# Weight narrowing moved from GpSimd to VectorE at other paces, and the sums of squares placed behind the last score product, in a channel-attention and GELU feed-forward kernel

## The chip, the cores and the metric

The kernel runs on one core of one Trainium2 chip. The metric is the time of one execution in microseconds (us) of device time; shorter is better. A core has TensorE (PE, matrix products; PEld is its loading of weights), VectorE (DVE), ScalarE (ACT), GpSimd (POOL) and SyncE (SP), which issues all DMAs of this kernel. Each engine works through its own queue of instructions in order.

## The reference

```python
def _attn_ref(q, k, v, tau):                      # each (4, 6080, 256)
    qn = q / (np.linalg.norm(q, axis=1, keepdims=True) + 1e-06)
    kn = k / (np.linalg.norm(k, axis=1, keepdims=True) + 1e-06)
    s = kn.transpose(0, 2, 1) @ qn / tau          # 256 x 256 per batch
    s = s - s.max(-1, keepdims=True)
    a = np.exp(s)
    a /= a.sum(-1, keepdims=True) + 1e-09
    return v @ a

def _moe_ref(x, w_in, w_out):                     # w_in 256 x 2048, w_out 2048 x 256
    h = x @ w_in
    g = 0.5 * h * (1.0 + erf(h / np.sqrt(2.0)))
    return g @ w_out
```

The attention runs over the 256 channels, so the scores are 256 x 256 per batch, and the norms are taken over the 6080 tokens. Its output, 24320 rows of 256, goes through the feed-forward layer. The weights arrive as 64-bit floats.

## The kernel before, in words

**Stages.** For each of 4 batches there is a score stage, a softmax, and 6 pairs of token tiles of up to 512 columns. For a pair, 8 steps (u = 0 to 7) go over the 2048 hidden channels. The attention matrix is multiplied into `w_in` beforehand (`w_group`, four groups g of 512 hidden channels, 12 products each), so that a step takes the tokens of `v` directly. Almost all products work on a high and a low part of each operand (`wh` and `wl`, `vh` and `vl`, `gh` and `gl`), three products each.

**A step.** `first_products` (lines 448 to 450) makes seven products of three matmuls; their results are copied by ScalarE (`p` and `u`, line 468), added by VectorE (`h`, line 473), and go through ScalarE's GELU twice (`gh` and `g`, lines 456 and 457), and VectorE takes the low part (`gl`, line 458). `second_products` (lines 518 to 520) multiplies the step's result with `w_out`; the second products of step u run between the first products of step u+1. TensorE does 21 + 24 matmuls in a step.

**The score stage of batch 0.** 24 loads `raw` of keys and queries (512 KB each, 13 buffers) come from `qk`, with the 24 sets of score products in `qk_first` (line 147, four matmuls of two passes each). For the first 16 of them ScalarE squares the load (`sq`, line 136, two buffers) and VectorE adds it to `acc` (line 137). The rest of the sum of squares comes from 8 pieces of the transposed keys and queries (`kqt`, line 211, three buffers), squared and summed by ScalarE (line 212). SyncE issues all of these loads from one queue in the order of the program, so a load that waits for its buffer holds up those behind it. Eight small matmuls against a column of ones (`sum_up`, line 175) add `acc` over the partitions. Four loads of batch 1 follow, and their score products (`qk_fill`, line 164) are what TensorE does in the gaps of the first softmax; `GAPS` says how many in each gap.

**The narrowing.** The 16 units of the weights (8 of `w_in`, 8 of `w_out`, 128 x 512 each) are turned from 64-bit floats into a high and a low part by integer and float operations on the two 32-bit words (`narrow`, lines 237 to 258): a clip (line 237, VectorE), a square (239, ScalarE), shifting and joining of the bits (242, 244, VectorE), a masked product (246, VectorE), an exponent mask (249, VectorE), the tail from the low word, the high part `hi` (256, ScalarE's copy), and the rest `lo` (257 and 258). Of these GpSimd does lines 257 and 258 for every unit, and line 255 of the tail for 12 units; for the other 4, VectorE makes the tail in one operation (line 251). Five units are narrowed in or right behind the score loop (`NARROWS`), though the order that comes out has two of these in the first softmax; one more follows it, and ten are spread over the first pair's steps, as many behind each step as `paces` says. Each unit is then written to DRAM (`keep`, line 551) for the later pairs and batches, and its place in the load queue goes to the next unit's load.

**What sets the order.** The program is written in one order, and instructions are placed on each engine's queue by a scheduler with priorities; `behind(...)` makes an instruction come after a marked one.

Of the kernel before, what the change touches and what calls it, by code (L numbers as in the profile page):

```python
# [9 lines left out]
F32 = mybir.dt.float32  # L10
F32R = mybir.dt.float32r
U32 = mybir.dt.uint32
AF = mybir.ActivationFunctionType
ALU = mybir.AluOpType
AX = mybir.AxisListType

P = 128
B, N, C = 4, 6080, 256
DFF = 2048
NT = 512  # L20
NJ = -(-N // P)
NFT = DFF // P
NCT = C // P
# [21 lines left out]
NARROWS = (4, 7, 12, 18, 20)  # L45

GAPS = (7, 4, 2)

VEC = 3

TOP_MAX = (2.0 - 2.0 ** -3 - 2.0 ** -23) * 2.0 ** 16
TOP_MIN = 1.125 * 2.0 ** -15
# [6 lines left out]
def channel_attention_gelu_ffn(ctx, tc, qk, kqt, vt, tau, w_in, w_out, out):  # L59
# [30 lines left out]
    def f32(ap):  # L90
        return ap.bitcast(F32)
# [48 lines left out]
    def qk_first(js):  # L140
        if js == 0:
            state["s"] = [bank()[:, 0:C] for m in range(NCT)]
        s = state["s"]
        raw = raws.pop((0, js))
        for j in range(JS):
            for m in range(NCT):
                nc.tensor.matmul(s[m], raw[:, j, 0, m * P:(m + 1) * P], raw[:, j, 1],
                                 start=(js == 0 and j == 0), stop=(js * JS + j == NJ - 1), skip_group_check=True)
        if js < NSQ:
            squares(js, raw)  # L150
        if js == NSQ + 2:
            nps, acc = ps_o.tile([P, NT], F32, name="po"), state.pop("acc")
            for j in range(JS):
                sum_up(nps, acc[:, j], j == 0, j == JS - 1)
            state["nps"] = nps


    def qk_fill():
        state["fill"] = s = ps_o.tile([P, NCT, C], F32, name="po")
# [61 lines left out]
        nc.sync.dma_start(out=raw, in_=src.bitcast(U32).rearrange("p (n w) -> p n w", w=2))  # L221
        return raw

    def narrow(hi, lo, raw, eng):


        n = raw.shape[1]
        low, high = raw[:, :, 0], raw[:, :, 1]

        if "filled" not in state:  # L230
            tmp = pst.tile([P, 2, n], F32, name="nt", bufs=2)
        else:
            tmp = pg.tile([P, 2, n], F32, name="kqc", bufs=2)

        top = high.bitcast(F32)
        body, w, tail = tmp[:, 0].bitcast(U32), tmp[:, 0], tmp[:, 1]
        nc.vector.tensor_scalar(out=top, in0=high.bitcast(F32), scalar1=TOP_MAX, scalar2=-TOP_MAX,
                                op0=ALU.min, op1=ALU.max)
        nc.scalar.activation(out=tail, in_=top, func=AF.Square)

        topu = top.bitcast(U32)
        nc.vector.tensor_scalar(out=body, in0=topu, scalar1=0x07FFFFFF, scalar2=3,
                                op0=ALU.bitwise_and, op1=ALU.logical_shift_left)
        nc.vector.scalar_tensor_tensor(out=topu, in0=topu, scalar=0xC0000000, in1=body,
                                       op0=ALU.bitwise_and, op1=ALU.bitwise_or)
        nc.vector.scalar_tensor_tensor(out=w, in0=tail, scalar=TOP_MIN ** 2, in1=top, op0=ALU.is_ge, op1=ALU.mult)

        body = high
        nc.vector.tensor_scalar(out=body, in0=w.bitcast(U32), scalar1=0xFF800000, scalar2=None, op0=ALU.bitwise_and)
        if eng is nc.vector:  # L250
            eng.scalar_tensor_tensor(out=tail, in0=low, scalar=2.0 ** -52, in1=body.bitcast(F32), op0=ALU.mult,
                                     op1=ALU.mult)
        else:
            nc.scalar.activation(out=tail, in_=low, func=AF.Copy, scale=2.0 ** -52)
            eng.tensor_tensor(out=tail, in0=tail, in1=body.bitcast(F32), op=ALU.mult)
        nc.scalar.copy(out=hi, in_=w)
        nc.gpsimd.tensor_tensor(out=w, in0=w, in1=f32(hi), op=ALU.subtract)
        nc.gpsimd.tensor_tensor(out=lo, in0=w, in1=tail, op=ALU.add)


    keep_in = [pdram.tile([P, 2, NCT, NT], F32, name=f"keep_in{g}") for g in range(NWG)]
# [23 lines left out]
    def softmax(first, pool, name):  # L285

        small = pm.tile([P, 32], F32, name="small")
        x, y, z, r = (small[:, 4 * i:4 * i + 4] for i in range(4))
        rk, nms, dens = (small[:, 16 + 2 * i:18 + 2 * i] for i in range(3))
        ts = []  # L290
        for m in range(NCT):
            t = pm.tile([P, C], F32, name=f"t{m}")
            if first:
                nc.scalar.copy(out=t, in_=state["s"][m])
            else:
                s = state["sacc"]
                nc.vector.tensor_tensor(out=t, in0=s[:, m, 0:C], in1=s[:, m, C:2 * C], op=ALU.add)
            ts.append(t)
        nsum = state.pop("nsum")
        if first:  # L300
            nc.vector.reduce_sum(out=z, in_=nsum[:, :, NSQ // NSJ:NSC], axis=AX.X)
            nc.vector.tensor_tensor(out=x, in0=state.pop("nps")[:, 0:2 * NCT], in1=z, op=ALU.add)
        else:
            nc.vector.reduce_sum(out=x, in_=nsum[:, :, 0:NSC], axis=AX.X)
        nc.vector.tensor_scalar(out=x, in0=x, scalar1=1e-30, scalar2=None, op0=ALU.max)
        yield

        nc.scalar.activation(out=y, in_=x, func=AF.Sqrt)
        if first:
            preload(AF.Exp, y)  # L310
        nc.vector.reciprocal(out=z, in_=y)
        nc.vector.tensor_tensor(out=z, in0=z, in1=x, op=ALU.mult)
        nc.vector.scalar_tensor_tensor(out=z, in0=z, scalar=2e-6, in1=y, op0=ALU.add, op1=ALU.add)
        nc.vector.reciprocal(out=r, in_=z)

        diag = pm.tile([P, NCT, P], F32, name="diag")
        nc.vector.tensor_tensor(out=diag, in0=ident.unsqueeze(1).broadcast_to([P, NCT, P]),
                                in1=r[:, NCT:2 * NCT].unsqueeze(2).broadcast_to([P, NCT, P]), op=ALU.mult)
        nc.vector.tensor_scalar(out=rk, in0=r[:, 0:NCT], scalar1=rtau, scalar2=4.0, op0=ALU.mult, op1=ALU.mult)
        yield  # L320
        rq = pool.tile([P, NT], F32, name=name)
        nc.tensor.matmul(rq[:, 0:C], ones, diag.rearrange("p h d -> p (h d)"), start=True, stop=True)
        for m in range(NCT):
            nc.vector.scalar_tensor_tensor(out=ts[m], in0=ts[m], scalar=rk[:, m:m + 1], in1=rq[:, 0:C],
                                           op0=ALU.mult, op1=ALU.mult)
            nc.vector.reduce_max(out=nms[:, m:m + 1], in_=ts[m], axis=AX.X, negate=True)
        yield
        es = []
        rden = pm.tile([P, 8], F32, name="rden", bufs=2)
        for m in range(NCT):  # L330
            e = pm.tile([P, C], F32, name=f"e{m}")
            den = dens[:, m:m + 1]
            nc.scalar.activation(out=e, in_=ts[m], func=AF.Exp, bias=nms[:, m:m + 1], accum_out=den)
            nc.vector.tensor_scalar(out=den, in0=den, scalar1=1e-9, scalar2=None, op0=ALU.add)
            nc.vector.reciprocal(out=rden[:, m:m + 1], in_=den)
            es.append(e)
        yield
        tp = pool.tile([P, NT], F32, name=name)
        tpv = tp.rearrange("p (d c) -> p d c", d=NCT)
        for m in range(NCT):  # L340
            for d in range(NCT):
                nc.tensor.transpose(out=tpv[:, d, m * P:(m + 1) * P], in_=es[m][:, d * P:(d + 1) * P],
                                    identity=ident)
        eh = pm.tile([P, NCT, C], F32R, name="eh")
        el = pm.tile([P, NCT, C], F32R, name="el")
        marks["eh"] = nc.scalar.copy(out=eh, in_=tpv)
        if first:
            preload(AF.Gelu, eh[:, 0, 0:2])
        marks["el"] = nc.vector.tensor_tensor(out=el, in0=tpv, in1=f32(eh), op=ALU.subtract)
        state["e"], state["rden"] = (eh, el), rden  # L350
# [199 lines left out]
        with behind("loads"):  # L550
            marks["kept"] = nc.sync.dma_start(out=dram, in_=f32(tile_))

    def narrow_unit(eng):
        kind, g, d, raw = loaded.popleft()
        if kind == "in":
            if d == 0:
                new_win(0, g)
            win = wins[0, g]
            narrow(win[:, 0, d], win[:, 1, d], raw, eng)
            if d == NCT - 1:  # L560
                keep(keep_in[g], win)
        else:
            new_wo((0, 0, g))
            wo = wos[0, 0, g]
            narrow(wo[:, 0].rearrange("p f c -> p (f c)"), wo[:, 1].rearrange("p f c -> p (f c)"), raw, eng)
            keep(keep_out[g], wo)

    preload(AF.Sqrt, ones)
# [1 line left out]
             ("in", 2, 0), ("in", 2, 1), ("out", 2, 0), ("out", 3, 0), ("in", 3, 0), ("in", 3, 1), ("out", 4, 0),  # L570
             ("out", 5, 0), ("out", 6, 0), ("out", 7, 0)]

    paces = (2, 1, 2, 2, 1, 1, 1)
    loaded = deque()


# [11 lines left out]
    for js in range(NQS):  # L588
# [5 lines left out]
        elif len(units) > 11:  # L594
            load_unit()
        if js in NARROWS:
            narrow_unit(nc.gpsimd)
        if js in (10, 11):
            v_sums(0, 0, js - 10)
        if 12 <= js < 19:  # L600
# [26 lines left out]
    for _ in fill:  # L627
        pass
    load_unit()
    narrow_unit(nc.gpsimd)  # L630
    load_unit()
    load_unit()

# [53 lines left out]
    for b, p, u in steps:  # L687
# [8 lines left out]
            pass  # L696
        if (b, p) == (0, 0):
            for _ in range(paces[u] if u < len(paces) else 0):
                narrow_unit(nc.vector if len(units) % VEC == 0 else nc.gpsimd)
                if units:  # L700
                    load_unit()
        extras(b, p, u)
# [31 lines left out]
```

## Time and profile before

| What | Value |
|---|---|
| Median of 3 runs | 2243.2 us (2242.62 to 2248.22) |
| The profiled execution's own time | 2243.63 us |
| Its span, first to last instruction | 2241.8 us |
| TensorE's mean granted clock | 0.992 |
| GpSimd's busy time, instructions | 77.1 us, 52 |
| Bytes moved | 269.63 MB, mean 120 GB/s |

Where rows of the profile are shown, a group of instructions reads: line, engine, operation, output from inputs, shape and type, count, then busy time in us and mean ns of one, then the engine's idle time ahead of them and who ended it. A row of the timeline begins with the start in us from the span's start and the duration. A row of waits names who waited for whom: us in total, times, longest. `<-` reads "from" or "released by". A product in fp32 runs as two passes, which the profile counts one by one.

### The profile page before, as it was taken

To read this page: it belongs to the slowest core of one execution; us is meant where nothing else is said; L and a number is where in the kernel's file an instruction comes from. 1 tells how busy PE (TensorE), PEld (TensorE's weight loads), DVE (VectorE), ACT (ScalarE), POOL (GpSimd) and SP (SyncE) were. 2 spreads that over 40 slices of the span, in tenths; PEclk is the share of its full clock that TensorE was granted. 3 is DMA by queue.
4 is the path that set the end of the run, shared out by engine and by line. 5 is a ranking of instruction groups with operands and counts; after the bars stand their busy time and mean duration, and the time that the engine had idled before them with its cause. 6 is when DMAs were issued, how large, how long until landed. Compare 5 with 4: busy or idle time off the path is not lost.

```text
span 2241.8 us, 26294 instructions
## 1 busy us (share of the span) xinstructions
PE 2190.7 (98%) x9640; PEld 1795.2 (80%) x9640; DVE 1410.7 (63%) x2161; ACT 1451.9 (65%) x2637; POOL 77.1 (3%) x52
## 2 busy tenths in 40 slices
PE   7889999999999999999999999999999999999999
PEld 5667777888888888888888888888888888888888
DVE  6698466675666766756567666576566655555454
ACT  6467887565985656656666556566576666666665
POOL 3351000000000000000000000000000000000000
PEclk9899999999999999999999999999999999999999
DMA  9446766331573323323224232232122221221221
GB/s 349 176 149 217 229 231 211 109 116 62 187 237 111 123 85 104 122 82 105 76 94 138 87 123 103 85 121 81 62 86 84 90 88 48 94 85 51 90 68 53
DMA packets 77634, 269.63 MB, mean 120 GB/s; under 512 B 7744, under 2 KB 9792, under 8 KB 75456
## 3 DMA queue, kind: packets, MB, share of 16 engines
q1 hardware_dynamic: 77504, 267.94, 35.2%
q8 instruction: 76, 1.25, 0.2%
q14 instruction: 54, 0.44, 0.1%
HBM read 234.62 MB, written 33.29 MB: 120 GB/s over the span
## 4 chain that ended last, share of the span: by engine, by line
PE 80%; ACT 6%; DMA 4%; DVE 4%; issue 1%; POOL 0%; ACTq 0%; DVEq 0%; POOLq 0%
PE po L520 14%; PE po L518 13%; PE po L519 13%; PE ph L450 12%; PE ph L449 12%; PE ph L448 12%; DMA kqc<-kqt 4%; PE ph L194 2%; ACT kqc L212 2%; ACT gh L456 1%; ACT g L457 1%; PE ph L196 1%; DVE gl L458 1%; DVE h L473 1%; PE ph L370 0%
## 5 line engine op out<-in xcount | busy, mean ns | idle before, releaser
L458 DVE TENSOR_TENSOR gl<-g,gh 128x512 fp32r<-128x512 f32 (+1 forms) x768 | 529.0, 691 | 155.8 <-ACT g L457 152.9
L520 PE MATMUL po<-gh,wo 128*128 128x512 f32 (+1 forms) x1536 | 605.7, 394 | 0.0
L519 PE MATMUL po<-gl,wo 128*128 128x512 f32 (+1 forms) x1536 | 597.2, 389 | 3.3 <-DVE gl L458 3.3
L518 PE MATMUL po<-gh,wo 128*128 128x512 f32 (+1 forms) x1536 | 598.3, 390 | 0.0
L473 DVE TENSOR_TENSOR h<-ph,p 128x512 f32<-128x512 f32 (+1 forms) x384 | 262.5, 684 | 529.3 <-PE ph L450 415.4
L456 ACT ACTIVATE gh<-h 128x512 fp32r<-128x512 f32 (+1 forms) x576 | 360.7, 626 | 298.6 <-DVE h L473 295.8
L448 PE MATMUL ph<-vh,wh 128*128 128x512 f32 (+1 forms) x1344 | 528.3, 393 | 21.2 <-DVE h L473 8.9
L450 PE MATMUL ph<-vh,wl 128*128 128x512 f32 (+1 forms) x1344 | 527.3, 393 | 1.8 <-DVE wl L355 1.0
L449 PE MATMUL ph<-vl,wh 128*128 128x512 f32 (+1 forms) x1344 | 526.4, 392 | 0.0
L468 ACT COPY p<-ph 128x512 f32<-128x512 f32 (+1 forms) x384 | 222.4, 583 | 250.7 <-PE ph L450 250.4
L457 ACT ACTIVATE g<-h 128x512 f32<-128x512 f32 (+1 forms) x576 | 352.5, 612 | 0.0
L519 PEld LDWEIGHTS po<-gl,wo 128*128 128x128 f32 x1536 | 288.9, 188 | 69.6 <-DVE gl L458 5.6
L520 PEld LDWEIGHTS po<-gh,wo 128*128 128x128 f32 x1536 | 289.0, 188 | 61.4
L518 PEld LDWEIGHTS po<-gh,wo 128*128 128x128 f32 x1536 | 288.5, 188 | 61.8 <-ACT gh L456 0.6
L448 PEld LDWEIGHTS ph<-vh,wh 128*128 128x128 f32 x1344 | 253.5, 189 | 85.4 <-DVE h L473 13.3
L449 PEld LDWEIGHTS ph<-vl,wh 128*128 128x128 f32 x1344 | 253.8, 189 | 56.0
L450 PEld LDWEIGHTS ph<-vh,wl 128*128 128x128 f32 x1344 | 253.4, 189 | 54.4 <-DVE wl L355 1.4
L468 ACT COPY u<-ph 128x512 f32<-128x512 f32 (+1 forms) x192 | 111.6, 581 | 116.5 <-PE ph L450 116.5
L473 DVE TENSOR_TENSOR h<-ph,u 128x512 f32<-128x512 f32 (+1 forms) x192 | 131.1, 683 | 3.4
L457 ACT ACTIVATE g<-ph 128x512 f32<-128x512 f32 (+1 forms) x192 | 111.8, 582 | 0.0
L456 ACT ACTIVATE gh<-ph 128x512 fp32r<-128x512 f32 (+1 forms) x192 | 110.2, 574 | 0.0
L194 PE MATMUL ph<-hl 128*128 128x512 f32 x272 | 96.0, 392 | 0.0
(135 smaller groups left out, 1399.4 us busy)
## 6 DMA issues: line engine op xcount, KB each, us to landing
wo<-keep_out SPq DMA_DIRECT2D x184, 512.0 KB, 3.3
raw<-qk SPq DMA_DIRECT2D x95, 512.0 KB, 4.4
kqc<-kqt SPq DMA_DIRECT2D x72, 512.0 KB, 4.5
v_raw<-vt SPq DMA_DIRECT2D x20, 1024.0 KB, 5.0
out<-osb SPq DMA_DIRECT2D x40, 512.0 KB, 3.2
win<-keep_in SPq DMA_DIRECT2D x12, 1024.0 KB, 5.0
kq<-kqt SPq DMA_DIRECT2D x8, 512.0 KB, 7.6
raw<-w_out SPq DMA_DIRECT2D x8, 512.0 KB, 4.1
```

Source lines behind the costliest of these rows:

```text
L194: nc.tensor.matmul(s, hl[:, 0, j, 0, cs], hl[:, :, j, 1], start=(i == 0), stop=False, skip_group_check=True)
L448: nc.tensor.matmul(ps[:, :n], wh, hi[:, :n], start=start, stop=False, skip_group_check=True)
L449: nc.tensor.matmul(ps[:, :n], wh, lo[:, :n], start=False, stop=False, skip_group_check=True)
L450: nc.tensor.matmul(ps[:, :n], wl, hi[:, :n], start=False, stop=stop, skip_group_check=True)
L456: nc.scalar.activation(out=gh[:, :n], in_=src, func=AF.Gelu)
L457: nc.scalar.activation(out=g[:, :n], in_=src, func=AF.Gelu)
L458: nc.vector.tensor_tensor(out=gl[:, :n], in0=g[:, :n], in1=f32(gh[:, :n]), op=ALU.subtract)
L468: nc.scalar.copy(out=t[:, :n], in_=ps[:, :n])
L473: nc.vector.tensor_tensor(out=h[:, :n], in0=ps[:, :n], in1=t[:, :n], op=ALU.add)
L518: nc.tensor.matmul(o, wo[:, 0, i, cs], gh[:, :n], start=first, stop=False)
L519: nc.tensor.matmul(o, wo[:, 0, i, cs], gl[:, :n], start=False, stop=False)
L520: nc.tensor.matmul(o, wo[:, 1, i, cs], gh[:, :n], start=False, stop=last)
```

## The change

It makes three edits.

1. In `qk_first`, the eight `sum_up` matmuls no longer stand behind load `NSQ + 2`. They go into the first `softmax`, placed behind the mark `scores`, which is the last score product.
2. `narrow` no longer uses GpSimd: VectorE makes the tail of all 16 units in one operation, and the two last operations of each unit, the subtraction and the addition. ScalarE's operation of the tail (line 254) goes for 12 units. In the changed kernel the tail is line 243, and the two others are lines 246 and 247.
3. `paces`, the number of units behind steps 0 to 6 of the first pair, becomes (1, 2, 1, 2, 2, 1, 1) from (2, 1, 2, 2, 1, 1, 1).

```diff
             for m in range(NCT):
-                nc.tensor.matmul(s[m], raw[:, j, 0, m * P:(m + 1) * P], raw[:, j, 1],
-                                 start=(js == 0 and j == 0), stop=(js * JS + j == NJ - 1), skip_group_check=True)
+                marks["scores"] = nc.tensor.matmul(
+                    s[m], raw[:, j, 0, m * P:(m + 1) * P], raw[:, j, 1],
+                    start=(js == 0 and j == 0), stop=(js * JS + j == NJ - 1), skip_group_check=True)
         if js < NSQ:
             squares(js, raw)
-        if js == NSQ + 2:
-            nps, acc = ps_o.tile([P, NT], F32, name="po"), state.pop("acc")
-            for j in range(JS):
-                sum_up(nps, acc[:, j], j == 0, j == JS - 1)
-            state["nps"] = nps
...
-        if eng is nc.vector:
-            eng.scalar_tensor_tensor(out=tail, in0=low, scalar=2.0 ** -52, in1=body.bitcast(F32), op0=ALU.mult,
-                                     op1=ALU.mult)
-        else:
-            nc.scalar.activation(out=tail, in_=low, func=AF.Copy, scale=2.0 ** -52)
-            eng.tensor_tensor(out=tail, in0=tail, in1=body.bitcast(F32), op=ALU.mult)
+        nc.vector.scalar_tensor_tensor(out=tail, in0=low, scalar=2.0 ** -52, in1=body.bitcast(F32), op0=ALU.mult,
+                                       op1=ALU.mult)
         nc.scalar.copy(out=hi, in_=w)
-        nc.gpsimd.tensor_tensor(out=w, in0=w, in1=f32(hi), op=ALU.subtract)
-        nc.gpsimd.tensor_tensor(out=lo, in0=w, in1=tail, op=ALU.add)
+        nc.vector.tensor_tensor(out=w, in0=w, in1=f32(hi), op=ALU.subtract)
+        nc.vector.tensor_tensor(out=lo, in0=w, in1=tail, op=ALU.add)
...
         if first:
+            nps, acc = ps_o.tile([P, NT], F32, name="po"), state.pop("acc")
+            with behind("scores"):
+                for j in range(JS):
+                    sum_up(nps, acc[:, j], j == 0, j == JS - 1)
             nc.vector.reduce_sum(out=z, in_=nsum[:, :, NSQ // NSJ:NSC], axis=AX.X)
-            nc.vector.tensor_tensor(out=x, in0=state.pop("nps")[:, 0:2 * NCT], in1=z, op=ALU.add)
+            nc.vector.tensor_tensor(out=x, in0=nps[:, 0:2 * NCT], in1=z, op=ALU.add)
...
-    paces = (2, 1, 2, 2, 1, 1, 1)
+    paces = (1, 2, 1, 2, 2, 1, 1)
...
-                narrow_unit(nc.vector if len(units) % VEC == 0 else nc.gpsimd)
+                narrow_unit()
```

The scheduler lays out the engines' queues anew: GpSimd's 44 operations of the narrowing are gone from its queue, and on the other engines the order differs from the score stage to the middle of batch 0. Three places of it stand in the prediction.

More of the change, by code (lines that the diff above doesn't have):

```diff
@@ L47 @@
 GAPS = (7, 4, 2)
-VEC = 3
 TOP_MAX = (2.0 - 2.0 ** -3 - 2.0 ** -23) * 2.0 ** 16
@@ L222, in load_w, with narrow @@
         return raw
-    def narrow(hi, lo, raw, eng):
+    def narrow(hi, lo, raw):
         n = raw.shape[1]
@@ L551, in keep, with narrow_unit @@
             marks["kept"] = nc.sync.dma_start(out=dram, in_=f32(tile_))
-    def narrow_unit(eng):
+    def narrow_unit():
         kind, g, d, raw = loaded.popleft()
@@ L558, in narrow_unit @@
             win = wins[0, g]
-            narrow(win[:, 0, d], win[:, 1, d], raw, eng)
+            narrow(win[:, 0, d], win[:, 1, d], raw)
             if d == NCT - 1:
@@ L564, in narrow_unit @@
             wo = wos[0, 0, g]
-            narrow(wo[:, 0].rearrange("p f c -> p (f c)"), wo[:, 1].rearrange("p f c -> p (f c)"), raw, eng)
+            narrow(wo[:, 0].rearrange("p f c -> p (f c)"), wo[:, 1].rearrange("p f c -> p (f c)"), raw)
             keep(keep_out[g], wo)
@@ L596, in channel_attention_gelu_ffn @@
         if js in NARROWS:
-            narrow_unit(nc.gpsimd)
+            narrow_unit()
         if js in (10, 11):
@@ L629, in channel_attention_gelu_ffn @@
     load_unit()
-    narrow_unit(nc.gpsimd)
+    narrow_unit()
     load_unit()
@@ L698, in channel_attention_gelu_ffn @@
             for _ in range(paces[u] if u < len(paces) else 0):
-                narrow_unit(nc.vector if len(units) % VEC == 0 else nc.gpsimd)
+                narrow_unit()
                 if units:
```

## The prediction

> **What bounds the kernel now.** I read the page first, then TensorE's waits, then windows over the stages in which those waits lie.
>
> ```profile
> span 2241.8 us, 26294 instructions
> PE 2190.7 (98%) x9640; PEld 1795.2 (80%) x9640; DVE 1410.7 (63%) x2161; ACT 1451.9 (65%) x2637; POOL 77.1 (3%) x52
> ```
> ```profile
> PE po L175 <- DVE acc L137: 9.5, 1, 9.5
> PE ph L448 <- DVE h L473: 8.9, 3, 6.3
> PE ph L147 <- DMA raw<-qk: 7.0, 5, 3.6
> ```
> TensorE is the bound of the whole: 98% busy. What can be won is in its waits, and the largest is one wait of 9.5 us, for VectorE's running sum of squares. The windows (us; busy time and count of PE, PEld, DVE, ACT, POOL; granted clock; DMA) say where TensorE is not the bound:
>
> ```profile
> 9.60:51.20 41.60, 29.84 (x127) 24.31 (x125) 39.05 (x42) 29.37 (x43) 17.61 (x9) 0.94 0.96 371
> 51.20:69.80 18.60, 18.48 (x73) 16.30 (x74) 1.74 (x9) 4.03 (x8) 0.00 (x0) 0.76 1.02 396
> 75.78:186.00 110.22, 86.49 (x325) 63.77 (x324) 100.92 (x151) 70.72 (x127) 55.23 (x33) 0.91 0.38 131
> 75.78:204.00 128.22, 104.49 (x403) 78.46 (x402) 116.10 (x172) 84.95 (x155) 58.15 (x35) 0.92 0.40 136
> 240.00:400.00 160.00, 155.83 (x686) 124.83 (x685) 103.23 (x158) 130.48 (x246) 0.00 (x0) 1.00 0.69 226
> ```
> Undisturbed, a matmul pass costs TensorE 155.83/686 = 0.227 us. The 403 passes from 75.78 to 204 would take 91.5 us at that pace; the stage lasts 128.2, and VectorE is busy for 116.1 of it. So VectorE sets the end of two stages: the scores (9.6 to 51.2, 39.05 of 41.6 busy) and the narrowing beside the first pair's eight steps (75.78 to 204). After 204 TensorE is the bound, so what is saved ahead of it reaches the end.
>
> **Part 1: the sums of squares behind the last score product.** TensorE's order before:
>
> ```order
> -L147 MATMUL ph<-raw_185 128x256 x4
> -L147 MATMUL ph<-raw_194 128x256 x4
> -L175 MATMUL po<-ones,acc 128x1 x8
> -L147 MATMUL ph<-raw_206 128x256 x4
> -L147 MATMUL ph<-raw_228 128x256 x4
> ```
> And with the change:
>
> ```order
> +L145 MATMUL ph<-raw_280 128x256 x4
> +L145 MATMUL ph<-raw_292 128x256 x4
> +L168 MATMUL po<-ones,acc 128x1 x8
> +L157 MATMUL po<-raw_307 128x256 x4
> +L157 MATMUL po<-raw_318 128x256 x3
> +L315 MATMUL po<-diag,ones 128x256
> ```
> The 8 sums (16 passes) move from behind the 17th load of scores to behind the 24th and last, ahead of the next batch's scores (L157) that fill the softmax's gaps. TensorE's timeline of before (start, duration, line, passes):
>
> ```profile
> 29.03 12.75 PE L147 MATMUL ph<-raw 128*128 128x256 f32 x56 [0.56 <-DMA raw<-qk]
> 51.32 3.54 PE L175 MATMUL po<-ones,acc 128*128 128x1 f32 x16 [9.54 <-DVE acc L137]
> 54.72 15.06 PE L147 MATMUL ph<-raw 128*128 128x256 f32 x56
> 69.62 3.19 PE L164 MATMUL po<-raw 128*128 128x256 f32 x14
> ```
> TensorE stops at 41.78 and has the last score at 69.78. Without the stop the remaining 56 passes would take 12.75 us, as the 56 before them did, and end at 54.5, if their data are there. The loads' side:
>
> ```profile
> SPq L211 <- ACT kq L212: 13.4, 4, 5.1
> ```
> ```profile
> 49.53 2.68 SPq L121 DMA_DIRECT2D raw<-qk  x5
> ```
> ```profile
> raw<-qk SPq DMA_DIRECT2D x12, 512.0 KB, 7.7
> ```
> The last score load is the first of the five issued at 49.53, and lands about 7.7 later. SyncE's queue is held up by pieces of the transposed keys and queries (L211) that wait for ScalarE to square the piece three before; ScalarE's squares wait for VectorE to add the last but one (two buffers). So VectorE paces the loads too. VectorE's rows:
>
> ```profile
> 9.62 1.23 DVE L137 TENSOR_TENSOR acc<-acc,sq 128x1024 f32<-128x1024 f32 x1 [9.62 <-ACT sq L136]
> 10.76 0.42 DVE L237 TENSOR_SCALAR raw<-raw 128x512 f32<-128x512 f32 x1
> 15.12 2.21 DVE L137 TENSOR_TENSOR acc<-acc,sq 128x1024 f32<-128x1024 f32 x1 [0.30 <-ACT sq L136]
> 17.26 1.49 DVE L237 TENSOR_SCALAR raw<-raw 128x512 f32<-128x512 f32 x1
> 25.00 3.75 DVE L137 TENSOR_TENSOR acc<-acc,sq 128x1024 f32<-128x1024 f32 x2 [0.71 <-ACT sq L136]
> 34.49 0.68 DVE L436 TENSOR_TENSOR vl<-vs,vh 128x512 fp32r<-128x512 f32 x1
> 35.10 0.68 DVE L436 TENSOR_TENSOR vl<-v_raw,vh 128x512 fp32r<-128x512 f32 x1
> 45.15 6.02 DVE L137 TENSOR_TENSOR acc<-acc,sq 128x1024 f32<-128x1024 f32 x3 [0.63 <-ACT sq L136]
> ```
> Against 1.23 and 0.42 the slow rows lose 1.0, 1.1, 1.3 and 2.3: 5.7 us here, all while GpSimd narrows. Added are 3 instructions for each of 3 units at 0.60 us (the distance of 34.49 and 35.10, rounded): 5.4. The two cancel: I leave the loads where they were or up to 3 us earlier, and take 1.5. Last load landed at 49.53 - 1.5 + 7.7 = 55.7, its own 8 passes 1.8, sums up to 3.54 (that row ran at a cold clock; half of it at best): 61.0 at most, 59.3 at least. Against 69.78: **-10** (-8.8 to -10.5). The ends: loads not earlier, -7.3; TensorE never waiting and short sums, 54.5 + 1.8, -13.5.
>
> Does the sum's consumer come late instead? From the sums to the diagonal:
>
> ```profile
> 56.51 0.16 DVE L302 TENSOR_TENSOR small<-po,small 128x4 f32<-128x4 f32 x1
> 57.97 0.43 DVE L317 TENSOR_TENSOR diag<-ident,small 128x256 f32<-128x256 f32 x1
> ```
> 1.9 us, under the 14 filling passes (3.19) that stand between. Cover is 1.3 us; without it I would add the difference. VectorE's last add, 51.2 before, comes ahead of 56 in any of these cases, so the sums no longer wait.
>
> **Part 2: narrowing on VectorE.** VectorE's order before, at the first step's products (h), where a unit's last two operations aren't VectorE's:
>
> ```order
> -L244 SCALAR_TENSOR_TENSOR raw<-raw,kqc 128x512
> -L249 TENSOR_SCALAR raw<-kqc 128x512
> -L246 SCALAR_TENSOR_TENSOR kqc<-kqc,raw 128x512
> -L473 TENSOR_TENSOR h<-ph,p_604 128x512
> -L458 TENSOR_TENSOR gl<-g,gh 128x512
> ```
> With the change, ahead of the sixth step's products:
>
> ```order
> +L243 SCALAR_TENSOR_TENSOR kqc<-raw 128x512
> +L246 TENSOR_TENSOR kqc<-kqc,wo 128x512
> +L383 TENSOR_TENSOR hl<-hl 128x256
> +L247 TENSOR_TENSOR wo<-kqc 128x512
> +L385 TENSOR_TENSOR hl<-hl 128x256
> +L389 TENSOR_TENSOR wl_527<-hl,wh_526 128x768
> +L386 TENSOR_TENSOR hl<-hl 128x256
> +L466 TENSOR_TENSOR h<-ph,p_1191 128x512
> ```
> L243, L246 and L247 now stand in VectorE's queue, with the step's h behind them. 13 of the 16 units fall into this stage: 13 x 2 subtractions and additions, and 9 tails (4 were VectorE's already), 35 x 0.60 = +21.0 us of VectorE. What goes is the slowing by GpSimd; groups by line from 75 to 186, and the same ones where GpSimd does nothing (gl: after 200; L237, L242 and L244: the two units ahead, on raw_w; count | busy, mean ns):
>
> ```profile
> L458 DVE TENSOR_TENSOR gl<-g,gh 128x512 fp32r<-128x512 f32 x24 | 22.6, 953 | 0.2
> L244 DVE SCALAR_TENSOR_TENSOR raw<-raw,kqc 128x512 uint32<-128x512 uint32 x11 | 10.2, 928 | 0.0
> L473 DVE TENSOR_TENSOR h<-ph,p 128x512 f32<-128x512 f32 x12 | 8.1, 679 | 1.3 <-PE ph L450 1.3
> L242 DVE TENSOR_SCALAR kqc<-raw 128x512 uint32<-128x512 uint32 x11 | 8.0, 737 | 7.6 <-POOL wo L258 3.8 <-POOL win L258 3.7
> L237 DVE TENSOR_SCALAR raw<-raw 128x512 f32<-128x512 f32 x11 | 7.8, 714 | 0.0
> L251 DVE SCALAR_TENSOR_TENSOR kqc<-raw 128x512 f32<-128x512 uint32 x4 | 3.8, 958 | 0.0
> L423 DVE TENSOR_TENSOR vs<-v_raw,vs 128x512 f32<-128x512 f32 x1 | 1.8, 1815 | 0.0
> L419 DVE TENSOR_TENSOR vs<-v_raw 128x512 f32<-128x512 f32 x1 | 1.8, 1764 | 0.0
> L244 DVE SCALAR_TENSOR_TENSOR raw_w<-raw_w,nt 128x512 uint32<-128x512 uint32 x2 | 1.4, 686 | 0.3 <-ACT nt L239 0.3
> L242 DVE TENSOR_SCALAR nt<-raw_w 128x512 uint32<-128x512 uint32 x2 | 0.8, 423 | 0.0
> L237 DVE TENSOR_SCALAR raw_w<-raw_w 128x512 f32<-128x512 f32 x2 | 0.8, 422 | 0.0
> ```
> ```profile
> L458 DVE TENSOR_TENSOR gl<-g,gh 128x512 fp32r<-128x512 f32 x612 | 420.1, 688 | 124.3 <-ACT g L457 122.1 <-PE ph L450 0.3
> ```
> gl 24 x 0.265 = 6.4, L244 11 x 0.242 = 2.7, L242 11 x 0.314 = 3.5, L237 11 x 0.292 = 3.2, L251 4 x 0.27 = 1.1, vs 2 x 1.1 = 2.2: -19.1. h, which reads one operand from PSUM, is not slowed (679), so this is no slower clock of VectorE. The waits for GpSimd in the L242 row go too: -7.5. Sum: 21.0 - 19.1 - 7.5 = -5.6. Not shown by the trace are the smaller groups' slowing (a gain) and VectorE's new wait at L246 for ScalarE's hi (a cost). ScalarE's queue there:
>
> ```order
> +L461 COPY p_1191<-ph 128x512
> +L388 CAST wh_526<-hl 128x768
> +L245 CAST wo<-kqc 128x512
> +L461 COPY p_1200<-ph 128x512
> +L461 COPY u_1208<-ph 128x512
> +L245 CAST wo<-kqc 128x512
> ```
> The second hi stands behind copies that wait for TensorE's products, and VectorE's h behind that hi. Bounds: at the good end VectorE has no gap, 116.1 + 21.0 - 19.1 = 118.0 against 128.2, so -10.2, and the rest of its work is slowed alike: the quoted groups hold 67.1 us of the window's 100.92 and lose 19.1, 28%; the other 33.8 would lose 9.6, which makes -19.8 (108.4 is still above TensorE's 91.5). At the bad end each of 13 units waits for one operation of ScalarE, about 0.6 us, +7.8, which makes +2.2. I take **-10**, the middle but for a little: two things lie on the good side, that TensorE's waits for h (8.9) come where a unit has to end on GpSimd first, and that ScalarE loses 9 tails.
>
> The Trainium skill (SBUF — State Buffer, Who interferes with whom) says that the pair of ports is locked for a whole instruction and the loser blocks fully; the gl and h rows agree in kind (two operands in SBUF, or one). Taken to its end it makes rival 4.
>
> **The new paces** (1, 2, 1, 2, 2, 1, 1) move no work in or out of the stage. Before, every unit came a step ahead of its use, 45 passes or 10.2 us. Now the fifth of the output units is narrowed at the end of the fifth step, whose second products run within the sixth; its L247 is ahead of the sixth step's h in the order above. I cost this at nothing; without that cover TensorE would wait for up to the unit's own instructions, 8 of 0.4 to 0.7 us, some 4.
>
> **Sum.** -10 - 10 = -20 from the profiled execution's 2243.63 (1.8 over its span), which stands 0.4 above the median: 2223.6, or **2223** as a median. A measurement of this kernel tells about 0.3%, 6.7 us, from no change.
>
> **Rivals.**
> 1. VectorE stays saturated: slowing gone, but the waits at L246 eat it, second stage 0. Time 2233. For it: the ScalarE rows above; against: TensorE's waits for h lie at GpSimd's work. 0.15. By the Trainium skill (Perfetto Trace Analysis, Optimizing Scalar/DVE Operations) a saturated VectorE may well hand work even to GpSimd, the reverse of this change, though it warns that the two share a port.
> 2. The stop only moves: L246 holds up the adds of squares, these ScalarE's squares and the pieces of L211, so scores end some 5 later than I reckon, and stage two gives nothing: -5, 2238, no change. Against: in the score stage only three units run. 0.10.
> 3. Slower: hi lies behind copies of products at most units, VectorE waits for ScalarE, which waits for TensorE, which needs h behind it. From (20 + 6.7)/13 = 2.1 us a unit it is slower by over 0.3%; at 2.5 us, 32.5 in all, 2256. For it: the order above; against: there h itself needs those products. 0.05.
> 4. More returns: each of GpSimd's operations blocks VectorE for all its length, so its 55.23 us come back instead of 19.1. VectorE then needs 116.1 + 21.0 - 55.2 = 81.9, TensorE's 91.5 sets the stage, -36.7: 2196. Against: VectorE's slow rows lose 1.1 each, not GpSimd's length. 0.04.
>
> My forecast has 0.66. Its own ends, -13.5 - 19.8 and -7.3 + 2.2, make 2210 to 2238; both good ends at once are unlikely, so the range starts at 2213, and it ends at 2236, past rival 1. Faster (under 2236.5) 0.85: the forecast, and rivals 1 and 4. Same 0.10: rival 2. Slower 0.05: rival 3.
>
> **What would show it.** No wait of the sums for acc, and the softmax's first filling pass at about 60 instead of 69.6; gl near 690 ns and no GpSimd work after the start; the eighth step's end at about 184 instead of 204. I am wrong if VectorE's waits for ScalarE's hi add up to over 10 us, or if TensorE's waits for loads in the scores grow by as much as the 9.5 that go.

## The result, and the profile after

| | before | after |
|---|---|---|
| Median, lowest and highest (us) | 2243.57 (2242.62 to 2248.22) | 2209.55 (2208.77 to 2211.5) |
| The profiled execution's own time | 2243.63 | 2209.69 |
| Its span | 2241.8 | 2207.9 |

The ratio is 0.9846, 95% interval 0.9829 to 0.9863: the change is worth 34 us. The forecast was 2223 with a range of 2213 to 2236: it had the right sign and named the two savings, but the measured time lies below its range, 13 us under the forecast. The page of after:

```profile
span 2207.9 us, 26235 instructions
PE 2179.6 (99%) x9640; PEld 1787.3 (81%) x9640; DVE 1402.2 (64%) x2205; ACT 1444.0 (65%) x2625; POOL 1.3 (0%) x8
```
VectorE has 44 instructions more and is busy for 8.5 us less: that is the result in one row. TensorE's waits, over the whole span:

```profile
PE ph L145 <- DMA raw<-qk: 7.7, 6, 3.5
PE ph L363 <- DVE win L247: 4.2, 4, 2.0
...
PE ph L441 <- DVE h L466: 0.3, 1, 0.3
```
The 9.5 us for `acc` and the 8.9 us for `h` are gone but for 0.3; the waits for loads grew by 0.7 only. New is a wait of 4.2 for narrowed `w_in` in `w_group` (L363).

**The first stage.** TensorE's timeline (start, duration, line, passes):

```profile
28.83 26.26 PE L145 MATMUL ph<-raw 128*128 128x256 f32 x112 [0.57 <-DMA raw<-qk]
54.92 1.84 PE L168 MATMUL po<-ones,acc 128*128 128x1 f32 x16
56.63 3.27 PE L157 MATMUL po<-raw 128*128 128x256 f32 x14
```
The last 14 loads run as 112 passes without a stop, the sums take 1.84 instead of 3.54, and the first filling pass comes at 56.63 instead of 69.62. SyncE's and VectorE's timelines say why it is even ahead of the 59.3 to 61.0 that I had:

```profile
46.13 2.46 SPq L119 DMA_DIRECT2D raw<-qk  x5
```
```profile
42.33 1.22 DVE L135 TENSOR_TENSOR acc<-acc,sq 128x1024 f32<-128x1024 f32 x1
44.07 2.55 DVE L135 TENSOR_TENSOR acc<-acc,sq 128x1024 f32<-128x1024 f32 x2
```
```profile
62.50 0.41 DVE L230 TENSOR_SCALAR raw_w<-raw_w 128x512 f32<-128x512 f32 x1
```
The adds of squares take 1.22 each now, the last ends at 46.6 instead of 51.2, and the last score load is issued 3.4 us earlier (I took 1.5). The window up to that add:

```profile
9.40:46.60 37.20, 33.52 (x146) 26.58 (x145) 36.60 (x51) 27.39 (x39) 0.00 (x0) 1.00 1.02 406
```
VectorE does nine instructions more than in the same window before (x42) and is busy for 2.45 less. The narrowing of `raw_w`, with which the second stage begins, starts 13.3 us earlier (75.78 before).

**The second stage**, from there to the 32nd `gl` (the end of the eighth step). Windows of before, then of after (us; busy time and count of PE, PEld, DVE, ACT, POOL; clock; DMA):

```profile
75.78:204.22 128.44, 104.71 (x404) 78.63 (x403) 116.32 (x173) 85.17 (x155) 58.15 (x35) 0.92 0.40 136
```
```profile
62.50:175.92 113.42, 103.28 (x424) 79.12 (x424) 109.39 (x207) 80.89 (x152) 0.00 (x0) 0.97 0.49 171
```
The stage is 15.0 shorter. VectorE does 34 instructions more in it (the 35 that GpSimd did before and an `h`, a small one too, against a cast and two `hl` of 128x1024 that now come outside) and is busy for 6.9 less; its idle time falls by 8.1, from 12.1 to 4.0. It is still what sets the stage: 109.4 of 113.4. Its groups from 62.5 to 178 (count | busy, mean ns | idle ahead):

```profile
L451 DVE TENSOR_TENSOR gl<-g,gh 128x512 fp32r<-128x512 f32 x33 | 22.6, 685 | 1.5 <-ACT g L450 1.3
L466 DVE TENSOR_TENSOR h<-ph,p 128x512 f32<-128x512 f32 x18 | 12.2, 683 | 2.1 <-PE ph L443 2.1
L237 DVE SCALAR_TENSOR_TENSOR raw<-raw,kqc 128x512 uint32<-128x512 uint32 x11 | 7.5, 686 | 0.0
...
L243 DVE SCALAR_TENSOR_TENSOR kqc<-raw 128x512 f32<-128x512 uint32 x11 | 7.5, 682 | 0.0
...
L246 DVE TENSOR_TENSOR kqc<-kqc,wo 128x512 f32<-128x512 f32 x7 | 4.8, 682 | 0.0
L247 DVE TENSOR_TENSOR wo<-kqc 128x512 fp32r<-128x512 f32 x7 | 4.8, 681 | 0.0
L242 DVE TENSOR_SCALAR raw<-kqc 128x512 uint32<-128x512 uint32 x11 | 4.6, 421 | 0.0
L235 DVE TENSOR_SCALAR kqc<-raw 128x512 uint32<-128x512 uint32 x11 | 4.5, 420 | 0.0
```
`gl` went from 953 to 685 ns, L237 (before: L244) from 928 to 686, L235 (before: L242) from 737 to 420; `h`, with one operand in PSUM, stayed where it was. L246 shows no idle time ahead of it: VectorE never waits for ScalarE's `hi`.

**After it.** From the start of the 32nd `gl` to the same output copy (34.0 apart in the two traces, at 310 and 276) TensorE needs

```profile
203.53:310.00 106.47, 103.52 (x450) 82.08 (x449) 65.54 (x104) 90.98 (x172) 0.00 (x0) 1.00 0.72 237
```
```profile
175.24:276.00 100.76, 100.03 (x440) 80.82 (x439) 67.04 (x102) 85.26 (x162) 0.00 (x0) 1.00 0.77 254
```
in before and after: 5.7 less. At VectorE's mark TensorE is 10 passes further on (10 x 0.227 = 2.3), and its gaps behind it are 0.7 instead of 3.0; the last 1.2 is that a pass takes 0.227 there instead of 0.230, for which I have no cause. So the 34 us are 13.3 + 15.0 + 5.6.

### The profile page after: what moved, and what is told of

The parts are those of the page before. It is cut to its first block, busy times and chain, and to the rows that moved or that the text cites. A ratio compares the mean times of both kernels' runs of the same rounds, so it can differ in the third digit from the quotient of the medians.

```text
span 2207.9 us, 26235 instructions
## 1 busy us (share of the span) xinstructions
PE 2179.6 (99%) x9640; PEld 1787.3 (81%) x9640; DVE 1402.2 (64%) x2205; ACT 1444.0 (65%) x2625; POOL 1.3 (0%) x8
## 4 chain that ended last, share of the span: by engine, by line
PE 87%; ACT 5%; DMA 4%; DVE 3%; issue 1%; SPq 0%; ACTq 0%; DVEq 0%
PE po L513 15%; PE po L511 14%; PE po L512 14%; PE ph L443 13%; PE ph L441 13%; PE ph L442 13%; DMA kqc<-kqt 3%; PE ph L187 2%; ACT kqc L205 2%; PE ph L189 1%; ACT gh L449 1%; ACT g L450 1%; DVE acc L135 1%; DMA raw<-qk 1%; DMA v_raw<-vt 1%
## 5 line engine op out<-in xcount | busy, mean ns | idle before, releaser
L451 DVE TENSOR_TENSOR gl<-g,gh 128x512 fp32r<-128x512 f32 (+1 forms) x768 | 522.6, 682 | 158.1 <-ACT g L450 155.9
```

Of the source, the lines that this page charges most:

```text
L451: nc.vector.tensor_tensor(out=gl[:, :n], in0=g[:, :n], in1=f32(gh[:, :n]), op=ALU.subtract)
```

## The experiments

**Theory A** is the prediction's: two independent savings, one from the sums' place, one from VectorE being slowed by GpSimd's work on SBUF, whoever waits for that work. **Its rivals**: of the parts, that one of them, or the new paces (theory C), carries the gain; of the slowing, that what mattered was the chain of a unit, its last steps on a slow engine and VectorE's waits for them, and the slow rows only went along with it (theory B of the runs with GpSimd beside). Four kernels take the change apart, three test the slowing by itself, and three try to go further. Medians and ratios are taken beside those of the kernel before on the same chip. "Above after" compares with after's 2209.55, which was measured on another occasion; where the ratios give another difference, it is given too.

### sums_only

The kernel before, with edit 1 alone:

```diff
-        if js == NSQ + 2:
-            nps, acc = ps_o.tile([P, NT], F32, name="po"), state.pop("acc")
...
+            with behind("scores"):
```


> The sums of squares behind the last score product, narrowing and paces as before. Theory A (two gains that do not need each other): TensorE no longer stops at 41.8, the loads stay as late as before (last score load issued at 49.5), so the softmax's first filling pass comes at about 59.5 instead of 69.6 and the time falls by about 10, to 2231 to 2235. Theory B (the stop was only VectorE slowed by GpSimd, so moving the sums without freeing VectorE gives little): the time falls by less than 4, 2240 or more.

Measured: 2234.11 (2231.85 to 2237.65) beside 2243.03, ratio 0.9959 (0.9944 to 0.9974), or -8.9. TensorE's timeline:

```profile
51.50 3.72 PE L147 MATMUL ph<-raw 128*128 128x256 f32 x16 [2.16 <-DMA raw<-qk]
56.32 1.99 PE L147 MATMUL ph<-raw 128*128 128x256 f32 x8 [1.11 <-DMA raw<-qk]
58.15 1.84 PE L171 MATMUL po<-ones,acc 128*128 128x1 f32 x16
59.86 3.27 PE L160 MATMUL po<-raw 128*128 128x256 f32 x14
```
The filling passes begin at 59.86, in the forecast's 59.3 to 61.0, and the scores end on loads, as forecast. So part 1's step was right for the change alone. The further 3.2 us of after's first stage (56.63) belong to edit 2: with GpSimd idle the squares and the loads behind them come earlier (the five loads that begin with the last score load are issued at 48.75 here and at 45.82 in `narrow_only`). The second stage, from `raw_w` to the 32nd `gl`, keeps its length of 128.4 without edit 2:

```profile
65.73:193.82 128.09, 104.44 (x406) 79.41 (x406) 113.39 (x174) 85.14 (x157) 60.91 (x35) 0.92 0.46 160
```

### narrow_only

The kernel before, with edit 2 alone (the sums behind load `NSQ + 2`, the old paces).

> All narrowing on VectorE, the sums at their old place and the old paces. Theory A: the second stage gains its full 20 us, and of the first stage the half that comes from VectorE finishing the squares at about 46.6 instead of 51.2, so TensorE's wait for acc is 4 to 5 us instead of 9.5: 2213 to 2219. Theory B: with VectorE freed the wait for acc is almost gone (under 1 us) and the time is that of the whole change, 2208 to 2211.

Measured: 2220.38 (2216.93 to 2225.15) beside 2243.03, ratio 0.9903 (0.9887 to 0.992), or -22.7: 1 us above theory A's range; its rival there falls. TensorE's wait and timeline, and the second stage:

```profile
PE po L172 <- DVE acc L135: 4.0, 1, 4.0
```
```profile
46.45 3.54 PE L172 MATMUL po<-ones,acc 128*128 128x1 f32 x16 [4.04 <-DVE acc L135]
49.86 14.79 PE L145 MATMUL ph<-raw 128*128 128x256 f32 x56
64.49 3.19 PE L161 MATMUL po<-raw 128*128 128x256 f32 x14
```
```profile
70.64:185.75 115.11, 104.10 (x420) 79.36 (x419) 110.56 (x207) 80.58 (x149) 0.00 (x0) 0.96 0.40 144
```
Without GpSimd the wait for `acc` is 4.0 instead of 9.5, and the filling passes come 5.1 earlier with the sums where they were. The second stage is 13.3 shorter than before, so most of its gain is edit 2's. What follows that stage is shorter too: from the 32nd `gl` to the end this trace takes 2029.4, against 2037.6 before and 2042.1 in `sums_only`; these are single executions, which differ by some us. Edit 2 is the larger by far, over twice edit 1. The two sum to -31.6 of the 34; the rest is about the paces' size.

### paces_only and old_paces

The kernel before with the new paces, and the changed kernel with the old ones:

```diff
-    paces = (2, 1, 2, 2, 1, 1, 1)
+    paces = (1, 2, 1, 2, 2, 1, 1)
```


> Only the paces are new; GpSimd narrows and the sums stand where they stood. Theory A (paces cost and bring nothing by themselves): 2240 to 2247. Theory C (the gain of the second stage that I did not forecast comes from the even pace): 2236 or less.

> The whole change with the old paces. Theory A: within 3 us of the change, 2208 to 2213. Theory C (the even pace makes the part of the second stage's gain that I did not forecast, 10 us): 2216 to 2222.

Measured: the new paces alone 2245.56 (2243.93 to 2250.89, 10 runs), ratio 1.0014 (1.0005 to 1.0023): a loss of 2.5. The changed kernel with the old paces 2212.33 (2211.86 to 2212.86), ratio 0.986 (0.9846 to 0.9875), 2.8 above after; the runs of the two (taken at different times) do not overlap, though the intervals of their ratios do. The paces aren't the cause, theory C falls. They cost a little while GpSimd narrows, and seem to bring about as much once VectorE does.

### gpsimd_beside

The changed kernel; beside each of the 11 units that are narrowed after the softmax GpSimd makes three subtractions, 33 in all, as it had operations from 75.78 to 186 before, into an output buffer that is idle then. They leave nothing out, they are added work that nobody reads.

```diff
         nc.scalar.copy(out=hi, in_=w)
+        if "filled" in state:
+            if "sc" not in state:
+                state["sc"] = pg.tile([P, NCT, NT], F32, name="osb", bufs=2)
+            for i in range(3):
+                nc.gpsimd.tensor_tensor(out=state["sc"][:, 0, :n], in0=f32(hi), in1=f32(hi), op=ALU.subtract)
```


> The changed kernel, but at each of the 11 units that are narrowed after the softmax GpSimd also makes three subtractions of hi from hi (two inputs in SBUF, 128 x 512, as many as it made in this stage before) into a buffer that nothing reads in that time. VectorE's and TensorE's orders are those of the changed kernel, and nobody waits for GpSimd. Theory A (GpSimd's running slows VectorE's operations on SBUF by about 25 us over the stage, whatever it computes): gl in the stage back from 685 to 900 ns or more, h unchanged near 683, the time 15 to 25 us above the changed kernel's, 2224 to 2235. Theory B (the gain came from the waits for GpSimd's results and from the shorter chain of a unit; the slow rows went along with it): gl under 750 ns, the time at most 2 us above, under 2212. Between 2212 and 2224 both have a part.

Measured: 2229.87 (2227.33 to 2230.32), ratio 0.9927 (0.991 to 0.9943): 20 us above after, 18 by the ratios. The time is in theory A's range, and B falls. GpSimd's groups, VectorE's, and the window of the stage:

```profile
L252 POOL TENSOR_TENSOR osb<-wo 128x512 f32<-128x512 f32 x21 | 37.6, 1790 | 107.7 <-ACT wo L245 106.4
L252 POOL TENSOR_TENSOR osb<-win 128x512 f32<-128x512 f32 x12 | 25.7, 2145 | 15.7 <-ACT win L245 15.0
```
```profile
L456 DVE TENSOR_TENSOR gl<-g,gh 128x512 fp32r<-128x512 f32 x36 | 30.9, 860 | 0.2 <-ACT g L455 0.2
L471 DVE TENSOR_TENSOR h<-ph,p 128x512 f32<-128x512 f32 x18 | 12.1, 679 | 1.7 <-PE ph L448 1.7
...
L246 DVE TENSOR_TENSOR kqc<-kqc,wo 128x512 f32<-128x512 f32 x7 | 7.3, 1041 | 0.0
```
```profile
62.26:192.09 129.83, 109.13 (x425) 81.15 (x425) 127.76 (x207) 82.14 (x152) 63.33 (x33) 0.93 0.42 148
```
VectorE does the same 207 instructions in the same order and takes 129.8 instead of 113.4; `h` is untouched again. `gl` at 860 falls short of the 900 I had named; its window, to 200, holds four undisturbed ones, but in the stage alone it is 882, still short. VectorE's busy time grows by 18.4 and its idle time shrinks by 2.0. So work that nobody waits for gives back 16.4 us of the stage, 0.50 a subtraction, and some 20 us of the time.

### gpsimd_copies

As above, with copies instead of subtractions: one input in place of two.

```diff
-                nc.gpsimd.tensor_tensor(out=state["sc"][:, 0, :n], in0=f32(hi), in1=f32(hi), op=ALU.subtract)
+                nc.gpsimd.tensor_copy(out=state["sc"][:, 0, :n], in_=f32(hi))
```


> As the run with GpSimd's three subtractions at each of 11 units, but with three copies (one input in SBUF) in their place. Theory A1 (any GpSimd operation on SBUF slows VectorE for as long as it runs): gl at 900 ns or more again, the time in proportion to GpSimd's busy time. Theory A2 (only the share of GpSimd's own reading and writing counts, two operands read against one): about half to two thirds of the other run's loss. Theory B: under 2212.

Measured: 2212.5 (2211.56 to 2218.51), ratio 0.9858 (0.9842 to 0.9874): 3 us above after. GpSimd's and VectorE's groups, and the stage:

```profile
L252 POOL COPY osb<-wo 128x512 f32<-128x512 f32 x21 | 31.5, 1502 | 102.3 <-ACT wo L245 101.3
L252 POOL COPY osb<-win 128x512 f32<-128x512 f32 x12 | 25.6, 2137 | 17.7 <-ACT win L245 17.2
```
```profile
L456 DVE TENSOR_TENSOR gl<-g,gh 128x512 fp32r<-128x512 f32 x40 | 30.2, 756 | 1.2 <-ACT g L455 1.0
```
```profile
63.30:180.84 117.54, 105.24 (x425) 79.91 (x425) 115.11 (x207) 81.46 (x152) 57.19 (x33) 0.96 0.46 161
```
GpSimd is busy for nearly as long (57.2 against 63.3, though the profile's spans on GpSimd are rough), yet the stage loses a quarter of what it lost to the subtractions (117.5 long, 4.1 more than after; VectorE's busy time grows by 5.7). Both A1, in proportion to GpSimd's busy time, and A2, half to two thirds, are refuted. GpSimd's busy time isn't the price. The time stands beside theory B's bound (under 2212); it is `gpsimd_beside` that rules B out, not this run. What the number of operands changes inside the chip was not looked into.

### gpsimd_twice

Six subtractions a unit instead of three (`range(6)`).

> As the run with GpSimd's three subtractions at each of 11 units, which came 20 us above the changed kernel, but with six. Theory A (each subtraction takes about 0.6 us from VectorE while VectorE sets the pace): 66 of them, 20 us more again where VectorE is the bound, 2244 to 2252, as slow as the kernel before although nobody waits for GpSimd. Rival (one GpSimd operation in flight at most costs what it costs; past a point VectorE blocks GpSimd instead): under 2238.

Measured: 2257.78 (2256.63 to 2261.78) beside 2241.26, ratio 1.0078 (1.0062 to 1.0094): 48 us above after (52 by the ratios), and slower than the kernel before. GpSimd's groups, VectorE's from 62.5 to 200, and the stage:

```profile
L252 POOL TENSOR_TENSOR osb<-wo 128x512 f32<-128x512 f32 x42 | 57.7, 1375 | 107.2 <-ACT wo L245 104.3
L252 POOL TENSOR_TENSOR osb<-win 128x512 f32<-128x512 f32 x24 | 37.3, 1555 | 18.9 <-ACT win L245 17.2
```
```profile
L456 DVE TENSOR_TENSOR gl<-g,gh 128x512 fp32r<-128x512 f32 x25 | 26.4, 1059 | 4.0 <-ACT g L455 4.0
L471 DVE TENSOR_TENSOR h<-ph,p 128x512 f32<-128x512 f32 x14 | 9.5, 682 | 1.5 <-PE ph L448 1.5
```
```profile
63.46:224.76 161.30, 119.47 (x425) 86.65 (x425) 154.78 (x207) 82.58 (x152) 95.04 (x66) 0.86 0.35 125
```
The stage takes 161.3, 47.9 more than after: the second 33 subtractions cost 31.5, twice the first 16.4. The price isn't linear, which I hadn't expected (2244 to 2252). With six a unit, a subtraction takes GpSimd only 1.4 to 1.6 us by the profile's rough spans, and it is VectorE that loses. TensorE, starved, has a granted clock of 0.86 in this stage, against 0.93 with three a unit and 0.97 in after. That can be little of the 31.5: VectorE's busy time, from 127.8 to 154.8, makes 27.0 of it, with the same instructions and `h` still at 682, and idle time the other 4.5. Why the second 33 cost more than the first stays open.

### weights_early, gpsimd_clip and clip_early

Three attempts to get below after. In the first, the loads of the next two units are issued ahead of the filling loads, since VectorE is idle there: 3.52 busy (DVE) of 15.90 in after's window from 46.6:

```profile
46.60:62.50 15.90, 15.76 (x81) 13.28 (x80) 3.52 (x16) 5.75 (x14) 0.00 (x0) 1.00 1.02 398
```
```diff
+            if js + AHEAD == NQS:
+                load_unit()
+                load_unit()
...
-        elif len(units) > 11:
-            load_unit()
```


> The changed kernel with the two loads of weights that follow the score loop issued ahead of the four loads of the next batch's scores, so that VectorE, which is busy for only 3.5 of the 15.9 us from 46.6 to 62.5, can begin on their units before the softmax. Theory A (VectorE sets the end of the stage until 175, so work taken ahead of it is worth its own length): up to the 6 operations of two units, 2 x 2.9 us, earlier: 2203 to 2208. Rival (the filling products wait for their loads, which now come 1 to 2 us later, and what VectorE does early is in the softmax's way): 2209 to 2213.

Measured: 2207.46 (2203.54 to 2209.94), ratio 0.9828 (0.9814 to 0.9843). That is in theory A's range, and the stage ends at 173.5 instead of 175.9 in its trace.

In the second, the clip of the 11 units goes to GpSimd; the third has both:

```diff
-        nc.vector.tensor_scalar(out=top, in0=high.bitcast(F32), scalar1=TOP_MAX, scalar2=-TOP_MAX,
-                                op0=ALU.min, op1=ALU.max)
+        clip = nc.gpsimd if "filled" in state else nc.vector
+        clip.tensor_scalar(out=top, in0=high.bitcast(F32), scalar1=TOP_MAX, scalar2=-TOP_MAX,
+                           op0=ALU.min, op1=ALU.max)
```


> The changed kernel with the clip of the 11 units that are narrowed after the softmax (a tensor_scalar, one input) on GpSimd instead of VectorE, straight behind the unit's load. Theory A (an operation with one input costs VectorE some 0.1 us, as the copies did): VectorE gives up 11 x 0.34 = 3.7 us and loses 1, so 2206 to 2209. Rival (the strided clip on GpSimd holds VectorE like a subtraction, or its result comes late): 2210 to 2216.

> The clips on GpSimd and the two early loads of weights together. If each is worth what it promised alone (2 to 3 us): 2203 to 2207. If TensorE rather than VectorE has become the bound of the stage, or the clips cost what they save: 2207 to 2213.

Measured: 2211.04 (2209.34 to 2214.79), ratio 0.9869 (0.9853 to 0.9885), and 2207.67 (2206.81 to 2216.01), ratio 0.985 (0.9834 to 0.9867). GpSimd's clips:

```profile
L231 POOL TENSOR_SCALAR raw<-raw 128x512 f32<-128x512 f32 x11 | 16.8, 1529 | 128.7 <-DVE nt L236 64.8 <-DMA raw<-w_out 27.2 <-DMA raw<-w_in 22.1
```
The first is in its rival's range, the second in that of its second case. The clip on GpSimd shows no gain, and none of the three can be told from after: the interval of each overlaps after's 0.9829 to 0.9863. For the early loads alone the medians give 2 us and the ratios 4, neither clear of noise.

## Why the prediction was wrong in size

The forecast was -20, and the change gave -34. Of the 14 us between them 3.3 belong to part 1, 5.0 to part 2, and 5.6 lie behind the second stage, where the forecast had no term. Each of the three alone would have left the time inside the range; together they did not.

- **What bounds the kernel**: right. VectorE set both stages, and what was saved there reached the end.
- **Part 1, -10 (ends -7.3 and -13.5)**: right alone (-8.9; filling at 59.86). In the change it came out at 13.3, near the good end. The mis-sized term is "I leave the loads where they were or up to 3 us earlier, and take 1.5": they came 3.4 earlier. I had cancelled 5.7 of slowing, from the quoted rows alone, against 5.4 for nine added instructions. By the windows, 39.05 busy of 41.6 before and 36.60 of 37.2 after with nine instructions more, VectorE got 5.4 + 2.45 = 7.9 of slowing back, and 2.0 of idle time. The sums took 1.84, near the short end of my two values.
- **Part 2, "I take -10, the middle but for a little"**: this is the step that failed. The sum behind it, 21.0 - 19.1 - 7.5 = -5.6, put the slowing of the smaller groups at nothing ("not shown by the trace"), and the way from -5.6 to -10 was a guess between two ends. The smaller groups are in the same list from 75 to 186 as the quoted ones:

```profile
L355 DVE TENSOR_TENSOR wl<-hl,wh 128x256 fp32r<-128x256 f32 x7 | 3.8, 567 | 0.0
L420 DVE TENSOR_TENSOR vs<-v_raw 128x512 f32<-128x512 f32 x1 | 1.8, 1786 | 0.0
L379 DVE TENSOR_TENSOR hl<-hl 128x256 f32<-128x256 f32 x1 | 1.5, 1485 | 0.0
```
The same operations take 419, 687 and 425 in after. With L384, L436, L246 and L249 such rows lose 5.7 in the whole stage, and the quoted ones 19.1, as reckoned. The windows agree within 1: the work in VectorE's stage grew by 18.8 (the 35 operations, 21.0, less 2.2 for the other changes in what falls into it), its busy time fell by 6.9, so 25.7 of slowing went. Idle time fell by 8.1, where the sum had 7.5. That makes 18.8 - 25.7 - 8.1 = -15.0. So the mis-sized term is the slowing, 25.7 instead of 19.1. The good end, 28.7 of slowing, was too much: it gave the rest the quoted groups' 28%, though of the rest `h` with `u` is not slowed at all (677), and its 33.8 comes from the window, in which neighbouring rows overlap by 0.08, while the rest's rows add up to some 45 by themselves. That the good end less the 4.0 of idle time that is left, -15.8, comes near the measured -15.0 is luck: its slowing was 3.0 too much and its added work 2.2 too much, and the two offset each other.
- **The bad end**, 0.6 us a unit for ScalarE's `hi`, did not occur at all: no idle time ahead of L246. I read a danger from the order of ScalarE's queue alone. `hi` copies the product of L239, and VectorE still has L242 and L243 to do before L246, 1.1 us by their rows; that this is what gave ScalarE its time is argued, not tested.
- **What no term held**: 5.6 us behind the stage. I ended the account at VectorE's mark, but before, TensorE trailed by 10 passes and had 2.2 us more of gaps behind that mark. The forecast's "what is saved ahead of it reaches the end" is right; what it left out is that the backlog goes as well.
- **The paces, 0**: about right, under 3 us either way.
- **"I am wrong if"**: neither came. VectorE's waits for `hi` are nil, and TensorE's waits for loads grew by 0.7. What went wrong lay on the side that I had not made a condition for.
- **Rivals**: 1 is out (the stage did get shorter), 2 too (the squares end 4.6 earlier, not 5 later), 3 too (no waits for `hi`). Rival 4 had the sign of the error but not the size: the stage is 113.4, not 91.5, and VectorE still sets it; the copies show that GpSimd's length is not what VectorE loses.

The causes shown by runs are these: GpSimd's subtractions slow VectorE with nobody waiting for them (16.4 us of the stage for 33), more of them cost more, and the sums' place is worth 9 us without the rest. The Trainium skill (SBUF — State Buffer, Who interferes with whom) lets a VectorE instruction with two inputs in SBUF contend with any GpSimd instruction that reads SBUF, the loser blocking fully. The subtractions agree (`gl` 860 and 1059, `h` 679 and 682); the copies read SBUF as well, and there VectorE lost 0.12 us each in the stage (4.1/33), so that both read SBUF does not by itself set what VectorE loses. Nor is it only instructions with two inputs that are slowed, as I read the `gl` and `h` rows: L237 and L242 have one, and the prediction's rows have them at 714 and 737 against 422 and 423. The same skill (Perfetto Trace Analysis, Optimizing Scalar/DVE Operations) would let a saturated VectorE hand work even to GpSimd, with a warning of the shared port; here the warning decides: taking over GpSimd's 35 operations in the stage brought VectorE 21.0 us of work, and 25.7 of slowing and 8.1 of idle time went.

## What to carry to other kernels

An engine that helps a saturated one can cost it more than it takes over: add up the excess of every row of the saturated engine over the same row in a quiet part of the trace, for the whole stage and not only for the largest groups, before you call the help a gain. Price the smaller rows from their own excess: here they were worth 5.7 us, and neither nothing, as in the sum, nor the large rows' share, as at the good end (9.6), was right. And follow a saving past the mark where it is made to the engine that comes next, whose backlog goes too.

## What the runs showed of the hardware

A GpSimd copy of 128x512 cost VectorE 0.12 us of the stage and a subtraction of that size 0.50, though GpSimd was busy for 57.2 and 63.3 us with 33 of each. With 66 subtractions the second half cost VectorE's stage 31.5 us, twice the first (27.0 of it in VectorE's own busy time), while the single subtraction got shorter on GpSimd (2145 and 1790 ns with three a unit, 1555 and 1375 with six). VectorE's addition `h`, with one input from PSUM, kept its length in all of these runs (677 to 684 ns). Operations with two inputs in SBUF did not (`gl`), nor did the clip and the shift with a single input there (714 and 737 ns beside GpSimd, 422 and 423 without).
